# A second product from seven half-size block products, and x held as a ring, in a fused attention and feed-forward kernel

## The chip, the cores and the metric

The kernel runs on one core of one Trainium2 chip. The metric is the device time of one execution in microseconds (us). The engines of the core work side by side and follow each other through semaphores: TensorE (PE) multiplies matrices, VectorE (DVE) and ScalarE (ACT) work elementwise and read the accumulators, GpSimd (POOL) and SyncE (SP) issue most of the transfers. PEld in a profile is PE's weight load.

## The reference, cut to what matters

```
scores = q @ k.T / 8 + bias_table[bucket(|i - j|)]     # 8 batches, 8 heads, 576 positions, 64 wide
x      = softmax(scores) @ v                           # heads side by side: 4608 tokens x 512
h      = x @ w_in                                      # 4608 x 2048
g      = h + sin(alpha * h)**2 / (alpha + 1e-9)
out    = g @ w_out                                     # 4608 x 512
```

Inputs and output are float32; the kernel's operands on PE are float16, its sums float32.

## The kernel before

The work is a list of tasks that `_graph` makes, each with its engine, an estimated duration, what it depends on and what it writes out (`emit`). `_Plan.run` puts them in order, engine by engine. The order on each engine is given ahead of time: `LINE` is a list of task numbers that has been found beforehand, and `_Plan.run` only takes the next task of each engine from it. So each engine has a fixed queue, in which nothing overtakes. `OPT["scalar"]` names the tasks that run on ACT where either ACT or DVE could do them.

Attention goes batch by batch (t = 0 to 7) and head pair by head pair (p = 0 to 3). The two heads of a pair lie in the two halves of the partitions, and their score matmuls (`qk_t`, L1220) use the array as two half arrays of 64 rows that work at the same time. ACT takes the exponential of 1024 columns out of two accumulator banks (`exp_u`, L1228), DVE multiplies in the bias as exp(bias) (`band_t`, L1256), and PE forms the sum over v (`av_w`, L1266 and L1276), with a column of ones for the denominator. `norm` (L1286, L1287) divides, and x is turned to x^T, on PE for t = 0 and by a transposing DMA on SP for the others (`turn_x`, L1293), into the tile `xT`, which holds all 4608 tokens. k and q come in transposed too: for t = 0 and 1, and q of t = 2, by PE (`turn`, L1155) from a staging area that lies inside `xT`, later by transposing DMAs.

The feed-forward part goes by blocks of tokens, `blk`: six of 512, two of 480, one of 576. For each block there are 16 units (f = 0 to 15). A unit is four matmuls `w_in`^T x^T into an accumulator bank (`moe_in`, L1325; two banks for 576 columns), the sine on ACT (`moe_sin`, L1332), the square on ACT or DVE (`moe_sq`, L1337 or L1339), and the gate on DVE (`moe_g`, L1353), which adds h, writes g in float16 and frees the bank. g is kept in buffers of 512 tokens, three of them (`ng=3`).

The second product (`moe_out`, L1368) takes output tiles of 128 tokens in pairs. A tile needs 16 matmuls with 128 columns of g as weights and 512 columns of `w_out` streaming:

```python
r = slice(64 * (i ^ turn), 64 * (i ^ turn) + 64) if rows else slice(0, 128)
self.nc.tensor.matmul(out=c["mo"][i], lhsT=self.g[tau // 4][r, f, at:at + 128],
                      rhs=self.w_out[r, f, :], start=i not in c["began"],
                      stop=True, skip_group_check=True)
```

For the pairs and quarters of f named in `rows`, both tiles are worked on at once, each on one half of the array, so that the array has the same shape as for the score matmuls around them; between the two turns of such a pair DVE touches both banks (`touch`, L1173). The 36 output tiles are copied to SBUF (`evict`, L1305 or L1307) and stored by SP (`store`, L1378).

## Time and profile before

| | us |
|---|---|
| median of 3 runs | 381.75 (381.33 to 381.82) |
| the profiled execution, its own time | 382.92 |
| its span (first to last instruction) | 381.1 |
| first matmul of the whole program | 4.56 |
| first matmul of the first product (block 0) | 35.00 |
| first matmul of blocks 6, 7, 8 | 277.64, 304.12, 329.61 |
| end of the last matmul | 377.44 |

The profile counts an engine as busy while at least one of its instructions runs. A mean per instruction includes its tail, which the next instruction on the engine may cover, so the start-to-start distance in a dense run is the better price; the timeline, which merges runs of equal instructions with their count, gives it. "x408" is a count of instructions.

### The profile page before, as it was taken

The page shows a single profiled execution, that of the slowest core. Times are in us where ns is not written, and L with a number is a line of the kernel's source. Part 1 is how long each engine was busy: PE and PEld are TensorE (multiplying, and loading weights), DVE is VectorE, ACT ScalarE, POOL GpSimd, SP SyncE. Part 2 cuts the span into 40 slices and gives each one's busy share as a digit, 9 for nine tenths or more (in the row PEclk, how much of TensorE's full clock was granted, in tenths as well). Part 3 has the DMA queues.
Part 4 walks back from the last instruction along what each step waited for, and adds up shares of the span by engine and source line. Part 5 has one row for each costly group of instructions (what it writes and reads, how often), then busy time and mean ns, then how long its engine had stood idle before and what let it go on. Part 6 is the DMA issues. An engine that isn't in the chain of part 4 may idle for free.

```text
span 381.1 us, 9520 instructions
## 1 busy us (share of the span) xinstructions
PE 369.9 (97%) x3939; PEld 201.3 (53%) x3939; DVE 268.3 (70%) x635; ACT 314.2 (82%) x419; POOL 88.2 (23%) x105
## 2 busy tenths in 40 slices
PE   4999999999999999999999999999999999999996
PEld 3566445756454556464655465546655545444442
DVE  4686988949964996579748974696569869668402
ACT  4788999899999999999999899997998686557311
POOL 8874651180028201910000008300000000000000
PEclk9999999999999999999999999999999999999999
DMA  8999999499939996997392049941710110210005
GB/s 158 203 157 153 176 186 125 81 148 148 173 82 147 162 158 82 183 157 167 43 182 79 3 96 154 108 67 23 160 58 17 37 37 19 72 57 3 0 2 220
DMA packets 148172, 40.82 MB, mean 107 GB/s; under 512 B 134416, under 2 KB 143456, under 8 KB 148128
## 3 DMA queue, kind: packets, MB, share of 16 engines
q0 software_dynamic: 96656, 18.45, 61.0%
q1 hardware_dynamic: 50768, 21.22, 27.8%
q8 instruction: 31, 0.51, 0.6%
q10 hardware_dynamic: 704, 0.53, 0.6%
q14 instruction: 13, 0.11, 0.1%
HBM read 36.94 MB, written 15.93 MB: 139 GB/s over the span
## 4 chain that ended last, share of the span: by engine, by line
PE 86%; DVE 5%; ACT 3%; DMA 3%; issue 1%; POOL 1%; ACTq 0%; POOLq 0%
PE acc L1368 31%; PE acc L1325 29%; PE acc L1276 10%; PE acc L1220 8%; PE acc L1266 3%; DVE g L1353 2%; ACT u L1228 2%; PE acc L1155 2%; DMA v<-in_v_dram 2%; DMA xT<-in_k_dram 2%; PE acc L1179 2%; PE acc L1210 1%; PE acc L1184 1%; DVE s L1339 1%; DVE xp L1287 1%
## 5 line engine op out<-in xcount | busy, mean ns | idle before, releaser
L1368 PE MATMUL acc<-w_out,g 128*128 128x512 f16 (+1 forms) x744 | 148.0, 378 | 0.6 <-DVE touched L1173 0.5
L1325 PE MATMUL acc<-xT,w_in 128*128 128x512 f16 (+2 forms) x640 | 134.7, 358 | 0.1
L1228 ACT ACTIVATE u<-acc 128x1024 f16<-128x1024 f32 x128 | 123.6, 1038 | 8.0 <-PE acc L1220 6.9
L1332 ACT ACTIVATE s<-acc,alphaT 128x512 f16<-128x512 f32 (+2 forms) x144 | 94.1, 684 | 24.4 <-PE acc L1325 18.2
L1353 DVE SCALAR_TENSOR_TENSOR g<-s,inv_a,acc 128x512 f16<-128x512 f16 (+4 forms) x176 | 107.5, 647 | 9.5 <-ACT s L1337 7.9
L1325 PEld LDWEIGHTS <-w_in 128*128 128x128 f16 x640 | 58.0, 98 | 66.1 <-issue 2.3
L1368 PEld LDWEIGHTS <-g 128*128 128x128 f16 (+1 forms) x744 | 51.2, 96 | 50.7 <-issue 8.4
L1256 DVE TENSOR_TENSOR u<-u,toep 128x1024 f16<-128x1024 f16 (+1 forms) x128 | 59.1, 487 | 26.6 <-ACT u L1228 26.5
L1035 POOL DMA_DIRECT2D v<-in_v_dram x32 | 33.3, 1116 | 91.8 <-PE acc L1276 85.1
L1220 PE MATMUL acc<-qT,kT 64*128 64x256 f16 x512 | 48.1, 285 | 0.5 <-DVE kT L1165 0.5
L1276 PE MATMUL acc<-v,u 128*128 128x65 f16 x1024 | 45.6, 195 | 0.1
L1337 ACT ACTIVATE s<-s 128x512 f16<-128x512 f16 (+2 forms) x70 | 43.2, 630 | 1.2
L1276 PEld LDWEIGHTS <-u 128*128 128x128 f16 x1024 | 41.5, 99 | 4.2 <-issue 0.2
L1307 DVE COPY outs<-acc 128x512 f32<-128x512 f32 x27 | 18.4, 687 | 27.7 <-PE acc L1368 27.2
L1339 DVE TENSOR_TENSOR s<-s 128x512 f16<-128x512 f16 (+2 forms) x74 | 30.2, 419 | 10.2 <-ACT s L1332 10.2
L1220 PEld LDWEIGHTS <-kT 64*128 64x128 f16 x512 | 22.0, 96 | 28.7 <-issue 16.3
L1287 DVE TENSOR_TENSOR xp<-acc,rden 128x256 f16<-128x256 f32 (+1 forms) x64 | 31.4, 491 | 2.4
L1266 PE MATMUL acc<-vt,ut 128*128 128x130 f16 x128 | 28.6, 224 | 0.0
L1041 POOL DMA_DIRECT2D vt<-in_v_dram x16 | 13.3, 832 | 51.8 <-PE acc L1179 27.3
L1305 ACT ACTIVATE outs<-acc 128x512 f32<-128x512 f32 x9 | 5.3, 603 | 18.4 <-PE acc L1368 18.4
L1228 ACT ACTIVATE ut<-acc 128x1024 f16<-128x1024 f32 x16 | 16.5, 1029 | 2.6 <-PE acc L1179 2.0
L1286 DVE RECIPROCAL rden<-acc 128x4 f32<-128x4 f32 (+1 forms) x64 | 11.8, 185 | 9.6 <-PE acc L1276 9.2
(70 smaller groups left out, 231.7 us busy)
## 6 DMA issues: line engine op xcount, KB each, us to landing
out_dram<-outs SPq DMA_DIRECT2D x36, 256.0 KB, 2.5
v<-in_v_dram POOLq DMA_DIRECT2D x32, 128.0 KB, 7.4
staged_k<-in_k_dram POOLq DMA_DIRECT2D x6, 576.0 KB, 11.1
staged_q<-in_q_dram POOLq DMA_DIRECT2D x5, 576.0 KB, 12.9
w_in<-in_moe_w_in_dram POOLq DMA_DIRECT2D x4, 512.0 KB, 8.8
w_out<-in_moe_w_out_dram POOLq DMA_DIRECT2D x4, 512.0 KB, 10.1
xT<-in_q_dram POOLq DMA_DIRECT2D x11, 144.0 KB, 6.5
xT<-in_k_dram POOLq DMA_DIRECT2D x7, 144.0 KB, 6.2
```

The source lines that it names most:

```text
L1220: self.nc.tensor.matmul(out=s[:, o:o + 256], lhsT=self.kT[t % 2][r, p, 128 * c:128 * c + 128], rhs=self.qT[t % 2][r, p, 256 * w:256 * w + ...
L1228: self.nc.scalar.activation(out=c["u"], in_=c["s"], func=AF.Exp, scale=0.125)
L1256: self.nc.vector.tensor_tensor(out=io, in0=io, in1=m, op=ALU.mult)
L1266: nc.tensor.matmul(out=c["av"][:, 130 * j:130 * j + 130], lhsT=tail, rhs=vt[:, p, :], start=True, stop=True, skip_group_check=True)
L1276: nc.tensor.matmul(out=c["av"][:, 130 * j + 65 * a:130 * j + 65 * a + 65], lhsT=l, rhs=vv[:, ch, 2 * p + a, 0:65], start=False, stop=True, ...
L1287: self.nc.vector.tensor_tensor(out=self.ap(x, 256 * w, [[64, n], [1, 64]]), in0=self.ap(av, 0, [[65, n], [1, 64]]), in1=self.ap(r, 0, [[1, ...
L1325: self.nc.tensor.matmul(out=c["h"][:, x:y], lhsT=self.w_in[:, j, 128 * f:128 * f + 128], rhs=self.xT[:, j, lo + x:lo + y], start=(j == 0), ...
L1332: self.nc.scalar.activation(out=c["s"], in_=c["h"], func=AF.Sin, scale=self.alphaT[:, f:f + 1])
L1337: self.nc.scalar.activation(out=c["s"], in_=c["s"], func=AF.Square)
L1339: self.nc.vector.tensor_tensor(out=c["s"], in0=c["s"], in1=c["s"], op=ALU.mult)
L1353: self.nc.vector.scalar_tensor_tensor(out=o, in0=c["s"][:, x:y], scalar=self.inv_a[:, f:f + 1], in1=c["h"][:, x:y], op0=ALU.mult, op1=ALU.add)
L1368: self.nc.tensor.matmul(out=c["mo"][i], lhsT=self.g[tau // 4][r, f, at:at + 128], rhs=self.w_out[r, f, :], start=i not in c["began"], stop ...
```

## The change

For the first eight of nine groups of 512 tokens the second product is formed by blocks. A group's g is 2048 x 512 and `w_out` is 2048 x 512; both are cut in halves in both directions, and the four quarters of the output (256 tokens x 256 columns) come from seven products of quarters instead of eight (Strassen's scheme, in the form with 4 sums on each side). One product is 8 values of f x 2 halves of 128 tokens, so 16 matmuls with 128 columns as weights and 256 columns streaming. The products are numbered; X, Y and Z are three accumulator banks:

- X gets product 1; Y gets product 2; the quarter 11 is X + Y.
- X goes on with product 6; Z gets products 5 and then 3; the quarter 12 is X + Z after both.
- X goes on with product 7; the quarter 22 is X + Z with only 5 in it.
- X goes on with product 4; the quarter 21 is X alone.

X is copied to SBUF after each of the four stages (`quarter`, on ACT or DVE), and the addition of Y or Z is an instruction of DVE on that copy (`quarter_sum`). Four sums of quarters of g are made for each group, in two instructions of 128 x 1024 each (`gate_sum`; two of the four are written over g), and four sums of quarters of `w_out` once (`weight_sum`). The ninth group is done as before, its four tiles one after the other.

To make room, `xT` becomes a ring of 4 x 576 = 2304 tokens, in which batch t writes over batch t - 4. The transposing DMA of x for t of 4 and later waits for the first-product matmuls that read the old tokens. The g buffers are two instead of three, the output buffers of `evict` two instead of three, and there are three buffers for quarters. Staging of q and k moves from `xT` to the tiles of the sums. Blocks are now seven of 512, one of 448 and one of 576; the block that crosses the end of the ring has its matmuls cut in two. `rows` is empty: no second product uses half arrays, and no touches are left. `LINE` is another list throughout, and `scalar` another set: 14 of the 32 copies of quarters are on ACT, of the four copies of the ninth group one is on DVE and three are on ACT, DVE has 84 squares instead of 74, and seven copies of transposed k and q move from DVE to ACT. The planner also knows longer durations for PE in the first 27 us. In the order of PE, five more groups of 12 transposes of q and k come before the first unit of block 0; in that of POOL, seven more loads of q and k, two of `w_out` and two of v come before the last two of `w_in`.

```diff
+XR = 4 * S
...
+        gone = [a for b, l in in_tasks.items() for a in l
+                if BLK[b][0] < S * (t - 3) + 64 and BLK[b][1] > S * (t - 4)] if t > 3 else []
+        tr = add("SP", 1.25, lambda: K.turn_x(xcell, t, p), deps=norms + gone, pipe=1.15, prio=0,
...
+        p1 = product(1, xu, state["fast"] + (in_tasks[bs[-1]][-1:] if bs[-1] == NBLK - 1 else []), g_of(0))
+        p2 = product(2, yu, [], g_of(1))
...
+        c11 = finish(11, p1, yu, p2)[0]
...
+        p5 = product(5, zu, [], both(1, 0))
+        p6 = product(6, None, [c11], both(2, 1))
+        c12 = finish(12, p6, zu, [])
+        p7 = product(7, None, [c12[0]], both(3, 2))
+        c22, q22 = finish(22, p7, zu, p5)
+        p4 = product(4, None, [c22], ww(3))
+        p3 = product(3, None, [q22], lambda f: s_of(4)(f))
+        c12[1].deps.extend(p3)
+        finish(21, p4, None, [])
...
-    line=_line(LINE), rows=((0,0), (0,3), (1,0), (1,1), (1,2), (1,3), (2,3), (3,0), (4,1), (4,3), (5,0), (5,3),
...
+    line=_line(LINE), rows=(), strict=False,
...
-    blk=(512, 512, 512, 512, 512, 512, 480, 480, 576),
+    blk=(512, 512, 512, 512, 512, 512, 512, 448, 576), fast=tuple(range(8)), split=False, p_sum=0.1,
...
-        self.xT = sgl.tile([128, NP, NT + 64], F16, name="xT")
+        self.xT = sgl.tile([128, NP, XR + 64], F16, name="xT")
...
+        self.sums = sgl.tile([128, 2, 2, NF // 2, 256], F16, name="sums")
+        self.wt = sgl.tile([128, 4, NF // 2, 256], F16, name="wt")
...
+        turn = -(-lo // XR) * XR - lo
+        if 0 < turn < n:
+            cuts = sorted({*cuts, turn})
+        for x, y in zip(cuts, cuts[1:]):
+            at = (lo + x) % XR
...
+    def weight_sum(self, i, k):
+        up, low = self.w_out[:, k:k + 4, :], self.w_out[:, k + 8:k + 12, :]
+        out = self.wt[:, :, k:k + 4, :]
+        a, b = ((up[:, :, 256:512], up[:, :, 0:256]), (low[:, :, 256:512], out[:, 0]),
+                (low[:, :, 256:512], up[:, :, 256:512]), (low[:, :, 0:256], out[:, 1]))[i]
+        self.nc.vector.tensor_tensor(out=out[:, i], in0=a, in1=b, op=ALU.subtract)
+
+    def gate_sum(self, c, i, n, k):
+        up, low = self.g[i][:, k:k + 4, :], self.g[i][:, k + 8:k + 12, :]
+        s = self.sums[:, i % 2, :, k:k + 4, :]
+        out, a, b = ((s[:, 0], up[:, :, 256:512], low[:, :, 256:512]), (s[:, 1], s[:, 0], up[:, :, 0:256]),
+                     (up[:, :, 256:512], up[:, :, 0:256], up[:, :, 256:512]),
+                     (low[:, :, 0:256], low[:, :, 0:256], s[:, 1]))[n - 1]
+        self.nc.vector.tensor_tensor(out=out, in0=a, in1=b, op=ALU.add if n == 1 else ALU.subtract)
+
+    def product(self, c, i, n, f0, bank):
+        to = {1: "X", 6: "X", 7: "X", 4: "X", 2: "Y", 5: "Z", 3: "Z"}[n]
...
+        for f in range(f0, f0 + 2):
+            u = f + NF // 2
+            a, b = {1: (g[:, f, 0:256], w[:, f, 0:256]), 2: (g[:, u, 0:256], w[:, u, 0:256]),
+                    5: (s[:, 0, f, :], t[:, 0, f, :]), 6: (s[:, 1, f, :], t[:, 1, f, :]),
+                    7: (g[:, f, 256:512], t[:, 2, f, :]), 4: (g[:, u, 256:512], t[:, 3, f, :]),
+                    3: (g[:, u, 0:256], w[:, u, 256:512])}[n]
+            for k in range(2):
+                self.nc.tensor.matmul(out=c[to][:, 256 * k:256 * k + 256], lhsT=a[:, 128 * k:128 * k + 128],
+                                      rhs=b, start=to not in c["began"], stop=True, skip_group_check=True)
...
+    def quarter(self, c, what, act):
+        c["o", what] = self.tp.tile([128, DM], F32, name="quarter", tag="quarter", bufs=3)
+        self.copy(c["o", what], c["X"], act)
+
+    def quarter_sum(self, c, what):
+        o, b = c["o", what], c["Y" if what == 11 else "Z"]
+        self.nc.vector.tensor_tensor(out=o, in0=o, in1=b, op=ALU.add)
```

236 lines of the change are left out of this document (192 added, 44 removed), and 116 rows, old and new, of the table LINE.

## The prediction

> **What bounds the kernel now.** I read the page first: the busy time of each engine.
>
> ```profile
> span 381.1 us, 9520 instructions
> ...
> PE 369.9 (97%) x3939; PEld 201.3 (53%) x3939; DVE 268.3 (70%) x635; ACT 314.2 (82%) x419; POOL 88.2 (23%) x105
> ```
>
> PE is busy for 97% of the span. A busy PE need not be a full one, so the timeline of PE comes next (columns: start, length of the merged run, engine, line, shapes, count); it says what a matmul costs in a stream.
>
> ```profile
> 35.00 10.30 PE L1325 MATMUL acc<-xT,w_in 128*128 128x512 f16 x47
> ...
> 101.88 0.39 PE L1220 MATMUL acc<-qT,kT 64*128 64x256 f16 x4
> 102.20 2.33 PE L1368 MATMUL acc<-w_out,g 128*128 128x512 f16 x10
> 104.47 0.39 PE L1220 MATMUL acc<-qT,kT 64*128 64x256 f16 x4
> 104.97 0.61 PE L1368 MATMUL acc<-w_out,g 64*128 64x512 f16 x4
> 105.41 0.38 PE L1220 MATMUL acc<-qT,kT 64*128 64x256 f16 x4
> 105.73 0.61 PE L1368 MATMUL acc<-w_out,g 128*128 128x512 f16 x2
> 106.27 0.61 PE L1220 MATMUL acc<-qT,kT 64*128 64x256 f16 x8
> 106.81 0.60 PE L1368 MATMUL acc<-w_out,g 128*128 128x512 f16 x2
> ...
> 107.31 0.41 PE L1276 MATMUL acc<-v,u 128*128 128x65 f16 x8
> 107.55 0.22 PE L1266 MATMUL acc<-vt,ut 128*128 128x130 f16 x1
> ```
>
> Three prices come out of it. The 47 matmuls of 512 columns take 10.30 us, the last one alone some 0.38 us, so they start every (10.30 - 0.38) / 46 = 0.2157 us. The eight of 65 columns start every (107.55 - 107.31) / 8 = 0.030 us. And a change of the array's shape costs about 0.1 us: from 102.20 to 104.47 ten matmuls at 0.2157 leave 0.11 us before the half-array score matmuls; from 105.41 to 105.73 four score matmuls, two at a time, need 2 x 0.109 = 0.22 us of the 0.32. Between the half-array pair of L1368 at 104.97 and the score matmuls at 105.41 there is no such loss: 0.44 us for two pairs. That is what the pairs of the kernel before are for.
>
> The stretches come third. I cut them where PE starts the first product of block 0 (35.00), block 6 (277.64) and block 8 (329.61).
>
> ```profile
> core 0: us, PE busy (x) PEld busy (x) DVE busy (x) ACT busy (x) POOL busy (x), PEclk, DMA share, GB/s
> 0.00:35.00 35.00, 28.42 (x455) 19.30 (x456) 23.76 (x70) 24.85 (x34) 24.98 (x45) 1.00 1.22 174
> 35.00:277.64 242.64, 241.70 (x2778) 132.45 (x2778) 181.19 (x419) 228.65 (x296) 63.26 (x61) 1.00 1.17 123
> 277.64:329.61 51.97, 51.97 (x431) 27.24 (x430) 41.53 (x101) 39.38 (x59) 0.00 (x0) 1.00 0.14 39
> 329.61:381.10 51.49, 47.83 (x277) 22.31 (x275) 21.85 (x47) 21.28 (x32) 0.00 (x0) 1.00 0.16 57
> ```
>
> From 35 us on PE has next to no gap: 0.94 us in the long middle, none after it, until its last matmul 3.7 us before the end. So the time from 35 us is PE's queue, matmul by matmul. But ACT is busy for 228.65 / 242.64 = 94% of the middle too, and only DVE has room there (75%).
>
> **The change, part by part.** I list the forms that carry the costs.
>
> ```profile
> L1368 PE MATMUL acc<-w_out,g 128*128 128x512 f16 x408 | 102.9, 380 | 0.5 <-DVE touched L1173 0.5
> L1353 DVE SCALAR_TENSOR_TENSOR g<-s,inv_a,acc 128x512 f16<-128x512 f16 x112 | 80.2, 743 | 1.2 <-ACT s L1337 0.4
> L1368 PE MATMUL acc<-w_out,g 64*128 64x512 f16 x336 | 45.2, 376 | 0.1
> L1256 DVE TENSOR_TENSOR u<-u,toep 128x1024 f16<-128x1024 f16 x64 | 43.3, 688 | 12.8 <-ACT u L1228 12.8
> L1276 PEld LDWEIGHTS <-u 128*128 128x128 f16 x1024 | 41.5, 99 | 4.2 <-issue 0.2
> L1339 DVE TENSOR_TENSOR s<-s 128x512 f16<-128x512 f16 x51 | 20.7, 420 | 3.8 <-ACT s L1332 3.7
> L1307 DVE COPY outs<-acc 128x512 f32<-128x512 f32 x27 | 18.4, 687 | 27.7 <-PE acc L1368 27.2
> L1287 DVE TENSOR_TENSOR xp<-acc,rden 128x384 f16<-128x384 f32 x32 | 17.8, 558 | 1.3
> L1287 DVE TENSOR_TENSOR xp<-acc,rden 128x256 f16<-128x256 f32 x32 | 13.6, 425 | 1.1
> L1165 DVE COPY qT<-acc 128x576 f16<-128x576 f16 x11 | 8.1, 752 | 6.2 <-PE acc L1155 6.2
> L1305 ACT ACTIVATE xT<-acc 128x320 f16<-128x320 f16 x3 | 1.2, 442 | 0.2 <-PE acc L1300 0.2
> L1163 ACT ACTIVATE kT<-acc 128x576 f16<-128x576 f16 x1 | 0.6, 634 | 0.0
> ```
>
> *Second product on PE.* Before: 408 full matmuls and 336 half-array ones in 168 pairs, so 576 slots of 0.2157 = 124.2 us. After: eight groups of seven products, each 16 matmuls of 256 columns, is 896, and 64 of 512 columns remain for the ninth group. The trace has no full-array matmul of 256 columns. Its price lies between half a 512 slot, 0.108, and a weight load on its own behind it, 0.108 + 0.099 = 0.207. I take the line through 512 columns (0.2157) and 65 columns (0.030): 0.415 ns a column, so 0.109 us, because the 65-column row shows a 128x128 weight load of 99 ns with each matmul and still one start every 30 ns. So 64 x 0.2157 + 896 x 0.109 = 111.5 us, **12.7 us less**.
>
> A rule speaks against this. The Trainium skill, "TensorE: Matmul & The Clock Gate", section "Back-to-back issue gap", gives for streams of weight load and matmul 81 ns at 128 columns and 131 ns at 512: halving a matmul would then save far less than half. On a line between these an estimate for 256 columns is 98 ns, and the sum would be 64 x 0.131 + 896 x 0.098 = 96 us after against 75 us before, 21 us more. This trace disagrees: 0.2157 us at 512 columns, and 0.030 us at 65.
>
> *Changes of shape.* The pairs are given up (rows is empty), so the products stand as full-array work between score matmuls. Counted in the two instruction orders, PE changes its tile shape 146 times before and 192 times after: 46 x 0.1 = **4.6 us more**. All on PE's queue.
>
> *Ring and blocks.* Block 4 crosses the end of the ring, so its 64 matmuls become 128 of 256 columns: 64 x (0.218 - 0.2157) = 0.15 us. Blocks of 480 and 480 become 512 and 448, the same columns. **0.2 us.** The transposed loads of x for t of 4 and later now wait for the matmuls that read the old columns; behind them on SP stand stores and later transposes. PE's order has those matmuls (blocks 0 and 1 for t = 4, up to block 4 for t = 7) one block or more ahead of the av that makes the new x, so this wait is over before it starts: nothing. Without that distance it would hold the next block's first matmuls.
>
> *Two g buffers for three.* A block's first matmul needs the products of the group two before. In PE's order they stand ahead of it, so PE waits for nothing new.
>
> PE's own queue, then: -12.7 + 4.6 + 0.2 = **-7.9 us**.
>
> *Work on DVE.* A row's mean holds a tail that the next instruction covers: in the next fence three gates take 2.06 us, so they start every (2.06 - 0.74) / 2 = 0.66 us where the mean is 0.743; I take 0.08 off each.
>
> ```profile
> 39.84 2.06 DVE L1353 SCALAR_TENSOR_TENSOR g<-s,inv_a,acc 128x512 f16<-128x512 f16 x3
> ```
>
> Added: 64 gate sums and 8 weight sums of 128x1024 f16, nearest row L1256 (0.688, so 0.60 to 0.69; I take 0.60), 43 us; 24 sums of a quarter with an accumulator, 128x512 f32, from the two L1287 rows 0.558 + 0.133 = 0.69, so 0.61 and 15 us. Removed: 8 of 27 copies (5 us), 7 turn copies to ACT (5 us), the nine touches and some split gates (3 us); 10 more squares come (3 us). About +48 us, from 268 to 316. None of it is on PE's chain as long as it is early: each X accumulator is copied out before the next product adds to it, and in PE's order 1.2 to 20 us of other work (mostly over 2 us, by the prices above) stand between a product's last matmul and the next one on X; the copy costs 0.69. Over six blocks the middle gets 48 gate sums, 8 weight sums and 16 quarter sums, less 8 copies and turns and the touches: +37 us, so 218 us. ACT's own list there hardly changes (139 sine and square instructions for 141, 104 exponentials for 106, 5 copies for 3, two turns), about -1 us. PE's work from block 0 to block 5, by the same prices over the two orders, falls by 5.4 us, so the middle would take 237 us: **DVE 92% busy, ACT 96%, PE near 100%**. That fits, but with a slack of 9 us on ACT and 19 on DVE where DVE had 61. I add **1.5 us** for waits this makes on PE, between none (0.94 us stood there at 94% and 75%) and the 17.6 us of the first rival.
>
> *The front.* Five full turn copies of 0.634 and two exponentials of 0.91 (from the next fence, 1.94 less one of 1.03) come ahead of ACT's first sine, three x copies of at most 0.44 go: 5 x 0.63 + 2 x 0.91 - 3 x 0.44 = +3.7 us by counts, against 35.00 - 24.85 = 10 us in which ACT was idle in the first stretch.
>
> ```profile
> 7.67 1.94 ACT L1228 ACTIVATE u<-acc 128x1024 f16<-128x1024 f32 x2
> ...
> 37.32 3.00 ACT L1332 ACTIVATE s<-acc,alphaT 128x512 f16<-128x512 f32 x5
> ```
>
> PE's front gains 2.0 us of work taken from block 0, which is in the sum already. So 0 to 2 us more is open on ACT. POOL's queue has more loads ahead of the last two of w_in, which is the third rival, up to 5 us. Between none and 5 I take **1 us**, nearer to none, since the idle time is there.
>
> *The end.* The stores write rows of half the length, as many bytes; only the last one shows, in the 3.7 us after the last matmul: 0 to 1 us.
>
> **Sum.** -7.9 + 1.5 + 1 = -5.4 us. The profiled execution has a span of 381.1 us and a time of 382.92, 1.2 above the median of the runs, 381.75. So 377.5 against its own time, and **376.4 us** against the median.
>
> **Rivals.** *The DVE queue sets the pace (slower).* Gates free the accumulators for the next first-product unit, and now a sum of 0.60 can stand ahead of a gate. If PE loses 0.2 us at each of the 64 gate sums and 24 quarter sums, that is 17.6 us: 381.75 - 7.9 + 17.6 = 391.5. It decides from 7.9 / 88 = 0.09 us for each. For it: 92% and 96% beside a full PE, no order is that even. Against it: 25% of DVE's middle was idle before and PE lost 0.94 us there with ACT at 94%. Chance 0.16.
>
> *Half-size matmuls don't cost half (slower).* If the weight load showed, 384 more loads x 0.098 = 38 us, so 412 us. The 65-column rows speak against it. Chance 0.01. By the Trainium skill, the same page, section "Part 3: Packing small matmuls", a weight load overlaps running matmuls only in another row group, which would make this so; the trace disagrees, with 30 ns between full-array matmuls.
>
> *Weights of the first product come late (smaller gain).* The DMA engines are full in these first slices of 9.5 us:
>
> ```profile
> DMA  8999999499939996997392049941710110210005
> GB/s 158 203 157 153 176 186 125 81 148 148 173 82 147 162 158 82 183 157 167 43 182 79 3 96 154 108 67 23 160 58 17 37 37 19 72 57 3 0 2 220
> ...
> w_in<-in_moe_w_in_dram POOLq DMA_DIRECT2D x4, 512.0 KB, 8.8
> ```
>
> ```profile
> 23.72 1.51 POOL L1046 DMA_DIRECT2D w_in<-in_moe_w_in_dram  x2
> ```
>
> Ahead of the last two w_in stand seven more loads of q and k of 144 KB, two of w_out of 512 KB and two of v of 128 KB: 2.3 MB, 14 us at 160 GB/s. The last w_in landed near 24.5 + 8.8 = 33.3 us; it is needed by the ninth unit, 8 x 0.86 us after 35, at 42. So 47.3 against 42: up to 5 us of PE in block 0, and 381.75 - 7.9 + 1.5 + 5 = 380.4, if none of these loads fills a gap. Chance 0.13.
>
> *Full gain.* The 2.5 us don't come and half or more of the 46 changes of shape cost nothing: 381.75 - 7.9 - 2.3 = 371.5 and below, down to 369.3 with all of them free. Chance 0.12.
>
> *No effect on the result.* Within 0.2% (about what a measurement of this kernel can tell from no change): gain and waits cancel. Chance 0.03.
>
> **Numbers.** The forecast, 372 to 379, has 0.55. Faster: 0.55 + 0.13 + 0.12 = 0.80; same 0.03; slower 0.17. The range goes from 369.5, the end of the full gain, to 383, the first rival with 0.1 us at each of 88 sums; the rest of the slower cases is left out.
>
> **What would show it.** Right: 896 matmuls of 256 columns starting every 0.109 us; PE busy in the middle still over 98%; DVE there above 90%; the first in-product at 35 to 39 us. Wrong: gaps on PE ahead of in-products released by DVE's gates or sums; ahead of products on X released by quarter copies; a w_in landing in PE's waits near 40 us; a spacing of 256-column matmuls well above 0.11 us.

## The result, and the profile after

The changed kernel takes 385.93 us (median of 6 runs, 384.31 to 387.76), the kernel before on the same chip 381.54 us (380.61 to 383.03). The ratio is 1.0118, with an interval of 1.0078 to 1.0157: 1.2% slower, where 376.4 was forecast, and outside the range of 369.5 to 383.0. The profiled execution has a span of 383.5 us and a time of 385.24. One run each of e1, e8 and e17 below fell into the slower of the chip's two states and is left out of their times.

The page of the changed kernel, its span and the busy time of each engine:

```profile
span 383.5 us, 10185 instructions
...
PE 361.8 (94%) x4219; PEld 241.8 (63%) x4219; DVE 316.8 (83%) x703; ACT 315.0 (82%) x421; POOL 88.5 (23%) x105
```

PE lost 8 us of busy time (369.9 before) and the span still grew by 2.4. So PE now waits. Cut at the first product of blocks 0, 1 and 2, the windows of the changed kernel (same columns as in the prediction):

```profile
0.00:39.09 39.09, 28.42 (x524) 20.27 (x524) 23.85 (x72) 28.77 (x38) 31.58 (x53) 0.91 1.19 161
...
39.09:87.35 48.26, 44.04 (x553) 26.27 (x554) 43.30 (x94) 45.76 (x58) 16.99 (x18) 1.00 1.35 144
87.35:128.22 40.87, 40.02 (x470) 26.19 (x469) 36.02 (x79) 37.04 (x48) 11.49 (x11) 1.00 1.39 143
128.22:383.50 255.28, 249.36 (x2677) 169.12 (x2675) 213.60 (x461) 203.38 (x280) 28.42 (x27) 1.00 0.66 85
```

and of the kernel before, cut at its own blocks 0, 1 and 2:

```profile
35.00:83.95 48.95, 48.64 (x653) 27.44 (x652) 37.68 (x86) 46.66 (x59) 25.64 (x27) 1.00 1.29 139
83.95:116.91 32.96, 32.85 (x374) 17.52 (x373) 26.23 (x63) 32.27 (x44) 5.70 (x7) 1.00 1.37 136
116.91:381.10 264.19, 260.02 (x2461) 137.05 (x2459) 180.66 (x420) 210.38 (x285) 31.92 (x30) 1.00 0.73 89
```

Before, PE is full from 35 us on. After, block 0 has 4.2 us without PE (0.3 before), block 1 has 0.85 (0.1 before), and block 0 starts 4.1 us later. The timeline of PE in the changed kernel names the gaps (idle before the row, and what ended it):

```profile
39.09 3.63 PE L1491 MATMUL acc<-xT,w_in 128*128 128x512 f16 x16 [0.52 <-DVE qT L1327]
...
47.85 3.61 PE L1491 MATMUL acc<-xT,w_in 128*128 128x512 f16 x16 [1.20 <-DVE g L1520]
51.74 4.48 PE L1491 MATMUL acc<-xT,w_in 128*128 128x512 f16 x20 [0.27 <-DVE g L1520]
...
57.89 1.03 PE L1571 MATMUL acc<-w_out,g 128*128 128x256 f16 x8 [0.45 <-DMA w_out<-in_moe_w_out_dram]
...
60.59 0.40 PE L1382 MATMUL acc<-qT,kT 64*128 64x256 f16 x4 [0.79 <-ACT ut L1390]
...
66.41 0.41 PE L1372 MATMUL acc<-qT,kT 64*128 64x64 f16 x16 [0.35 <-ACT u L1390]
...
68.25 0.39 PE L1382 MATMUL acc<-qT,kT 64*128 64x256 f16 x4 [0.40 <-ACT u L1390]
...
88.80 0.59 PE L1491 MATMUL acc<-xT,w_in 128*128 128x512 f16 x2 [0.85 <-DMA xT<-xp]
...
313.88 1.47 PE L1571 MATMUL acc<-wt,sums 128*128 128x256 f16 x12 [1.24 <-ACT quarter L1467]
...
340.15 1.15 PE L1491 MATMUL acc<-xT,w_in 128*128 128x512 f16 x8 [0.31 <-DVE g L1520]
341.56 2.13 PE L1491 MATMUL acc<-xT,w_in 128*128 128x512 f16 x16 [0.26 <-DVE g L1520]
...
372.83 1.91 PE L1571 MATMUL acc<-wt,g 128*128 128x256 f16 x16
```

The last row is the price that the forecast stood on: sixteen matmuls of 256 columns in 1.91 us; less the tail of the last one, 0.273 us (the mean of its form), that is (1.91 - 0.273) / 15 = 0.109 us from start to start.

**The account.** Counts times the prices of the prediction give PE 355.2 us of work before and 347.1 after: -8.1. Block by block, what a stage takes beyond PE's work in it is lost:

| us | PE's work, before | after | lost, before | after | change of the loss |
|---|---|---|---|---|---|
| up to block 0 | 17.9 | 19.9 | 17.1 | 19.2 | +2.1 |
| block 0 | 46.7 | 41.2 | 2.3 | 7.1 | +4.8 |
| block 1 | 32.5 | 39.5 | 0.5 | 1.4 | +0.9 |
| block 2 to the last matmul | 258.2 | 246.5 | 2.3 | 4.8 | +2.5 |
| behind it | | | 3.7 | 3.9 | +0.2 |
| sum | 355.2 | 347.1 | | | +10.5 |

-8.1 + 10.5 = 2.4, the growth of the span. Block 0 is the place: 5.5 us less of PE's work in it (2.0 of them moved ahead of it), and it takes 48.26 us instead of 48.95. Of its +4.8 us, 3.9 are idle time of PE (4.2 against 0.3). Half of the idle time, 2.08 us, stands ahead of rows released by a load or a gate. The other half, 2.07 us in six waits, ends with exponentials of ACT; before the change such waits came to 0.14 us.

**Two chains read back.** The gap at 47.85 ends with a gate. DVE's timeline shows what the gate stood behind:

```profile
45.79 0.69 DVE L1546 TENSOR_TENSOR wt<-w_out 128x1024 f16<-128x1024 f16 x1 [1.74 <-PE acc L1491]
46.40 0.75 DVE L1327 COPY qT<-acc 128x576 f16<-128x576 f16 x1
47.06 2.05 DVE L1520 SCALAR_TENSOR_TENSOR g<-s,inv_a,acc 128x512 f16<-128x512 f16 x3
```

The first weight sum needs the first and the third quarter of `w_out`. It also writes `wt`, which is now the staging area of q and k of t = 1 as well, so it must wait until PE has turned the last of them. The turns were done first: PE waits 0.16 us at 43.25 for their last load and is through with them at 43.95. The third quarter of `w_out`, issued at 33.77, landed at 45.71, and the sum starts at 45.79. POOL's queue, which waits for a landing of `w_out` too, shows both ends:

```profile
33.77 0.81 POOL L1212 DMA_DIRECT2D w_out<-in_moe_w_out_dram  x1
...
45.99 0.62 POOL L1202 DMA_DIRECT2D vt<-in_v_dram  x1 [1.74 <-DMA w_out<-in_moe_w_out_dram]
```

The copy of a turn and three gates wait behind the sum in DVE's queue. So the PE instruction in the sum's brackets is not what it waited for: the cause is a load, and behind it POOL's order of loads.

The gap at 313.88 ends with the copy of a quarter. ACT:

```profile
313.23 0.60 ACT L1467 ACTIVATE quarter<-acc 128x512 f32<-128x512 f32 x1 [1.87 <-PE acc L1491]
```

and SP's queue:

```profile
307.74 1.20 SPq L1455 DMA_TRANSPOSE xT<-xp  x1
309.00 2.97 SPq L1585 DMA_DIRECT2D out_dram<-quarter  x3
```

The copy needs a buffer, there are three, and the three stores that free them were issued behind a transposing load of x that could not go before its x was there. They took 4.1 to 4.2 us to land, the first of them until 309.0 + 4.2 = 313.2, which is when the copy starts.

### The profile page after: what moved, and what is told of

Its sections match the earlier page's. It is cut to its first block, busy times and chain, and to the rows that moved or that the text cites. A ratio compares the mean times of both kernels' runs of the same rounds, so it can differ in the third digit from the quotient of the medians.

```text
span 383.5 us, 10185 instructions
## 1 busy us (share of the span) xinstructions
PE 361.8 (94%) x4219; PEld 241.8 (63%) x4219; DVE 316.8 (83%) x703; ACT 315.0 (82%) x421; POOL 88.5 (23%) x105
## 3 DMA queue, kind: packets, MB, share of 16 engines
q1 hardware_dynamic: 54864, 21.22, 27.5%
## 4 chain that ended last, share of the span: by engine, by line
PE 74%; DVE 8%; DMA 7%; ACT 4%; POOL 3%; issue 2%; SPq 1%; ACTq 0%; DVEq 0%
PE acc L1491 28%; PE acc L1571 23%; PE acc L1438 8%; PE acc L1382 6%; PE acc L1535 4%; DVE g L1520 3%; ACT u L1390 3%; DMA wt<-in_q_dram 3%; PE acc L1428 2%; DMA toep<-e_sb 2%; DMA xT<-xp 1%; DMA cst_sb<-cst 1%; PE acc L1341 1%; DVE u L1418 1%; DVE s L1506 1%
## 5 line engine op out<-in xcount | busy, mean ns | idle before, releaser
L1491 PE MATMUL acc<-xT,w_in 128*128 128x512 f16 (+3 forms) x704 | 134.4, 340 | 3.4 <-DVE g L1520 2.0
L1520 DVE SCALAR_TENSOR_TENSOR g<-s,inv_a,acc 128x512 f16<-128x512 f16 (+2 forms) x160 | 105.7, 689 | 5.0 <-ACT s L1504 2.9
L1491 PEld LDWEIGHTS <-w_in 128*128 128x128 f16 x704 | 64.9, 98 | 59.4 <-issue 3.9
L1571 PEld LDWEIGHTS <-g 128*128 128x128 f16 x640 | 58.6, 98 | 21.2 <-issue 7.8
L1418 DVE TENSOR_TENSOR u<-u,toep 128x256 f16<-128x256 f16 (+1 forms) x128 | 58.8, 486 | 4.1 <-ACT u L1390 3.8
L1196 POOL DMA_DIRECT2D v<-in_v_dram x32 | 33.4, 1117 | 110.8 <-PE acc L1438 46.7
L1571 PE MATMUL acc<-w_out,g 128*128 128x256 f16 x384 | 52.5, 273 | 0.4 <-DMA w_out<-in_moe_w_out_dram 0.4
L1571 PE MATMUL acc<-wt,sums 128*128 128x256 f16 x256 | 35.2, 273 | 1.2 <-ACT quarter L1467 1.2
L1571 PE MATMUL acc<-wt,g 128*128 128x256 f16 x256 | 35.9, 273 | 0.0
L1382 PEld LDWEIGHTS <-kT 64*128 64x128 f16 x512 | 19.2, 96 | 19.1 <-issue 15.7
L1571 PEld LDWEIGHTS <-sums 128*128 128x128 f16 x256 | 23.2, 98 | 10.2 <-issue 5.0
L1581 DVE TENSOR_TENSOR quarter<-quarter,acc 128x512 f32<-128x512 f32 x24 | 16.3, 681 | 5.5 <-PE acc L1571 3.4
## 6 DMA issues: line engine op xcount, KB each, us to landing
staged_q<-in_q_dram POOLq DMA_DIRECT2D x5, 576.0 KB, 13.8
```

Of the source, the lines that this page charges most:

```text
L1196: self.nc.gpsimd.dma_start(out=self.vs[t % 2][:, c, :, 0:D], in_=src)
L1382: self.nc.tensor.matmul(out=s[:, o:o + 256], lhsT=self.kT[t % 2][r, p, 128 * c:128 * c + 128], rhs=self.qT[t % 2][r, p, 256 * w:256 * w + ...
L1418: self.nc.vector.tensor_tensor(out=io, in0=io, in1=m, op=ALU.mult)
L1491: self.nc.tensor.matmul(out=c["h"][:, x:y], lhsT=self.w_in[:, j, 128 * f:128 * f + 128], rhs=self.xT[:, j, at:at + y - x], start=(j == 0 a ...
L1520: self.nc.vector.scalar_tensor_tensor(out=o, in0=c["s"][:, x:y], scalar=self.inv_a[:, f:f + 1], in1=c["h"][:, x:y], op0=ALU.mult, op1=ALU.add)
L1571: self.nc.tensor.matmul(out=c[to][:, 256 * k:256 * k + 256], lhsT=a[:, 128 * k:128 * k + 128], rhs=b, start=to not in c["began"], stop=Tru ...
```

## The experiments

Ratios are against the kernel before on the same chip. A queue is shown by names, and the lines of the diff are its order. Every kernel changes only what is shown; e8, e9, e12, e13 and e15 also hold the accumulator banks of the tasks to a fixed list.

### Is it DVE's new work, and is PE still the pace?

```diff
 e3: gate_sum
-        self.nc.vector.tensor_tensor(out=out, in0=a, in1=b, op=ALU.add if n == 1 else ALU.subtract)
+        return
...
 product
-                    5: (s[:, 0, f, :], t[:, 0, f, :]), 6: (s[:, 1, f, :], t[:, 1, f, :]),
+                    5: (g[:, u, 256:512], t[:, 0, f, :]), 6: (g[:, f, 256:512], t[:, 1, f, :]),
 e4: product
-        for f in range(f0, f0 + 2):
+        for f in [x for x in range(f0, f0 + 2) for _ in range(2 if n == 5 else 1)]:
```

> The changed kernel without its 64 gate sums on DVE (38 us of DVE); products 5 and 6 read blocks of g itself in their place, so the output is not the network's. PE's list is the same. Theory A (the loss lies ahead of 87 us, PE's queue sets the pace behind it): DVE falls from 317 to about 278 us and the time by less than 1 us, to about 385. Theory B (DVE's new work holds PE back): the 6.2 us of PE gaps in blocks 1 to 8 fall to the 2.9 of the kernel before, so 382.5 or less.

> The changed kernel with an eighth product in each of the eight groups: the matmuls of product 5 are issued twice, so 128 more matmuls of 256 columns, and the output is not the network's. At the 0.109 us of the stream this is 14.0 us of PE. If PE's own queue sets the pace from block 0 on (theory A), all of it is seen: 385.9 + 14.0 = 399.9, between 399 and 401. If DVE sets the pace in part (theory B), some of the 14.0 us fills gaps that are there anyway: 3 us less or more, 397 or below.

e3: 386.05 us, ratio 1.0083 (1.0054 to 1.0111). Its page:

```profile
PE 361.9 (94%) x4219; PEld 242.0 (63%) x4219; DVE 280.6 (73%) x639; ACT 315.2 (82%) x421; POOL 87.9 (23%) x105
```

36 us of DVE's work are gone, and with them no time that can be told from noise (the interval overlaps that of the changed kernel). The first rival, the DVE queue, falls as far as the gate sums go; e3 leaves the quarter sums and the weight sums in. e4: 396.51 us, 1.0377 (1.0354 to 1.04). Its 128 added matmuls are 128 x 0.109 = 14.0 us of PE's work; the profiled span grew by 10.9. Most of what PE is given shows, so PE's pace still sets most of the time. Some 1.9 of the missing 3.1 us are gaps that the added work covers: the quarter at 313 us (1.24) and part of the wait for x^T (0.22 for 0.85). Another 0.6 us is a first unit that came earlier, which the edit does not explain. The start of the first unit moves between executions: with the same front it is 39.09 us in the changed kernel, 38.47 in e4, 39.18 in e3 and 39.64 in e14.

### One wait at a time

```diff
 e1: PE, front
-bias_sub, qk_t, qk_t, bias
+qk_t, qk_t, bias_sub, bias
 e2: DVE, block 0
-weight_sum (first), turn copy, gate, gate, gate, ..., sq0.15, weight_sum (second)
+turn copy, gate, gate, gate, ..., sq0.15, weight_sum (first), weight_sum (second)
 e5: POOL
-w_in (second quarter), ..., v, w_in (first quarter), v, w_out, q (t = 1), w_out, w_in, w_in
+w_in (first quarter), ..., w_in (second quarter), k and q (t = 1), w_in, w_in, w_out, w_out, v, v
```

> The changed kernel with one matmul moved: on PE the subtraction of the bias table (L1236), which waits 1.15 us for the landing of cst_sb, stands behind the first two groups of score matmuls instead of ahead of them. Theory A (the gain was lost in the front and in block 0, before 87 us): the first scores start near 6.5 us instead of 7.99, ACT's first exponential near 7.6 instead of 9.07, and the first product of block 0 starts up to 1.5 us earlier than 39.09; the time falls by 0.5 to 1.5 us from 385.9. Theory B (DVE's 48 us of new work holds PE back in blocks 1 to 8): the front gives at most what it gives and blocks 1 to 8 keep their 6.2 us of PE gaps; no more than 1 us. If the band tiles (toep), which come from the same bias chain, are what is late in the front, then this edit makes them later, and the time does not fall.

> The changed kernel with one DVE instruction moved: the first weight sum (L1546 at 45.79 us, which waits 1.74 us for the last turns of t = 1 to leave the tile wt) stands just ahead of the second weight sum, near 58 us. Theory A: the 1.20 us for which PE waits at 47.85 for a gate goes, with part of the 0.27 at 51.74; the time falls by 1.0 to 1.5 us from 385.9. If the gates are late for another reason (ACT's turn copies, w_in), the gap stays and the time changes by less than 0.3 us. Theory B expects no change outside block 0.

> The changed kernel with POOL's queue of loads in another order: the quarter of w_in that block 0 needs first (units 0 to 3) takes the place of the second quarter at 8.71 us; behind the copies of the mask (27.95 us) go first the rest of w_in and the last turns' loads of k and q for t = 1, then w_out, and v of t = 1, needed near 66 us, last. Nothing else moves. Theory A1 (the lost microseconds of block 0 are loads that land late): the waits of PE on wt<-in_q (0.16 us), on the gate behind the weight sum (1.20, which waited for that load), on w_out (0.45) shrink, 1.5 us less at the start of block 1. Theory A2 (each wait removed uncovers the next one, as in the two single moves before this): block 1's first x, the transposes of x for t = 1, still lands at 88.7 to 88.9 us, and the time stays within 0.7 us of 385.9.

e1: 384.86 us, 1.0065 (1.0046 to 1.0084). The first scores start at 6.97 us instead of 7.99, but the first sum over v at 26.40, where it was 26.34. The first unit starts at 38.21; that is not shown to be the edit's work, since e2, with the front as it was, has it at 38.22. Block 1 starts at 87.35 as before, since PE now waits for the load of q:

```profile
43.26 0.70 PE L1318 MATMUL acc<-ident,wt 96*64 96x96 f16 x24 [1.05 <-DMA wt<-in_q_dram]
```

e2: 385.84 us, 1.0093 (1.0076 to 1.0111). The gap of 1.20 us behind the gate is gone, and the two loads that it had covered show:

```profile
47.20 7.08 PE L1492 MATMUL acc<-xT,w_in 128*128 128x512 f16 x32 [0.70 <-DMA w_in<-in_moe_w_in_dram]
56.79 1.03 PE L1572 MATMUL acc<-w_out,g 128*128 128x256 f16 x8 [1.42 <-DMA w_out<-in_moe_w_out_dram]
...
88.66 0.59 PE L1492 MATMUL acc<-xT,w_in 128*128 128x512 f16 x2 [1.83 <-DMA xT<-xp]
```

Block 1's first product started at 86.24, 1.1 us earlier, 0.9 of them because the first unit did; block 0 itself is 0.24 us shorter. The next part of x^T landed at 88.66 (88.80 without the edit). e5: 391.27 us, 1.0244 (1.0215 to 1.0273), worse: `w_out` comes later now, the first weight sum needs its third quarter, and the gates stand behind that sum. DVE and PE of e5:

```profile
48.95 0.69 DVE L1547 TENSOR_TENSOR wt<-w_out 128x1024 f16<-128x1024 f16 x1 [4.57 <-DMA w_out<-in_moe_w_out_dram]
```

```profile
51.02 10.58 PE L1492 MATMUL acc<-xT,w_in 128*128 128x512 f16 x36 [4.78 <-DVE g L1521]
```

So the waits lie in layers: the one removed uncovers the next, and this order of loads is a loss as long as the sum stands early in DVE's queue.

### All of them together, and the stores

e6 is e5, e2 and e1 in one; e7 adds to it:

```diff
 SP, near 305 us
-turn_x (t = 7), store_quarter, store_quarter, store_quarter
+store_quarter, store_quarter, store_quarter, turn_x (t = 7)
 POOL
-staged k of t = 5, ..., two staged loads of t = 3
+two staged loads of t = 3, staged k of t = 5
```

> The order of loads of e5, and the two single moves of before (bias subtraction behind the first scores on PE, first weight sum later on DVE) with it. Theory A1: front -0.9 us, block 0 -1.2 for the gate and -1.5 for loads, so block 1 starts near 84 instead of 87.35; of that 1.5 to 3.5 us reach the end: 382.4 to 384.4. Theory A2: the transposes of x hold block 1 again, as PE's wait there grew from 0.85 to 1.83 us when 1.1 us went ahead of it; then 384.5 to 385.5.

> e6, and on SP the three stores of group 5 that wait behind a transpose of x for t = 7 (issued at 307.74, the stores from 309.00) go ahead of it, so that the quarter buffers come free; on POOL the staging load of k for t = 5 goes behind those of t = 3, out of the way of the transposes of x near 83 us. Theory (the 1.24 us for which PE waits for a quarter copy at 313 is a wait for a buffer whose store landed 4.2 us after its late issue, and not ACT's copy itself): that wait goes, 1.0 to 1.3 us below e6. If it is the copy itself (0.60 us on ACT, behind its exponentials), it stays.

e6: 384.52 us, 1.0083 (1.0056 to 1.0111), where e5 alone had 1.0244. Its block 0 takes 46.99 us, 1.3 less than in the changed kernel. PE's waits for loads and gates there fall from 2.08 to 0.66 us; those for exponentials stay, at 2.04. e7: 383.70 us, 1.0057 (1.0039 to 1.0075). SP of e7 issues the stores at once:

```profile
304.23 1.43 SPq L1586 DMA_DIRECT2D out_dram<-quarter  x3
307.61 1.20 SPq L1456 DMA_TRANSPOSE xT<-xp  x1
```

The gap in front of the quarter product is gone, and block 7 takes 28.40 us instead of 29.55 in e6 and 29.96 in the changed kernel. That chain is shown. It is not gone for good: e10 and e17 have a gap of this kind near 209 us (1.11 and 2.79 us), where the trace of the changed kernel has none.

### The front: copies, clock, and what holds it

```diff
 e8: e7, two turn copies from ACT to DVE
-scalar: ... turn0.1.1 turn0.3.0 ...
 e10: e7, PE, 17 to 25 us: 48 matmuls of 128 columns on the unit matrix into free banks
+fill x6 (ahead of each group of scores that waits for ACT)
 e11: e10 and 27 more ahead of the first transposes, the first scores and the bias product
 e12: e8 and e11, 6 more of these matmuls, and POOL and DVE in the front
-v, v, ..., band, mask, band
+..., v, v, mask, mask, band, band
 e13: e12, POOL
-staged loads of t = 3 behind v
+staged loads of t = 3 ahead of v
```

> e7, and in the front two of the turn copies (0.66 and 0.65 us at 10.9 and 13.1 us of the changed kernel) run on DVE, which idles there, instead of ACT, which is busy without a break from 12 to 25 us while PE waits 0.3 to 0.5 us at each of eight score groups for ACT's exponentials. Theory C (ACT's exponentials set the pace of the front, and the turn copies given to it lengthen them): ACT's stretch ends 1.3 us earlier, the first product of block 0 starts 0.8 to 1.3 us earlier, and as nothing behind block 1 waits for the front any more than before, 0.5 to 1.3 us reach the end: 382.4 to 383.2 at a median of 383.7 for e7. Theory D (the bands on DVE, which wait for the Toeplitz tiles and the masks, set the start of attention times v): the exponentials end earlier, the first matmul with v stays where it is, and so does the time, within 0.4 us.

> e7 with 48 empty matmuls of 128 columns (identity on identity, into a free bank, results unused) on PE in eight of the places where PE waits 0.3 to 0.5 us for ACT between 17 and 25 us, six at each. Theory E (PE's gaps of the front are what takes its clock to a half at about 20 us, for 6.8 us, in some runs for 10.2 us): the clock stays at 1.00 from 13.4 us on, the attention of t = 0 from 25 us on runs at full price sooner, and the first product of block 0 comes 0.5 to 1.5 us earlier; runs near 0.98 of mean clock no longer occur, so the spread of the times shrinks; 382.2 to 383.2. If the halved clock has another cause, it stays, and the time is that of e7, 383.7, or up to 0.5 us more.

> e10 with 27 more of the same empty matmuls ahead of PE's first transposes (from about 3 us, where PE idles until 4.9 to 5.7), ahead of the first scores and ahead of the bias product. Theory E: the clock is full from about 7 to 10 us instead of 13.4, so the transposes and scores up to 13 us, which PE does without a gap at half the speed, take up to 2 us less; ACT's exponentials start to follow each other sooner; the first product of block 0 comes 1 to 2 us earlier than in e7: 381.7 to 382.7. If ACT and the loads hold the front in any case, no gain over e10.

> All that was moved in the front at once: e11 (empty matmuls in PE's gaps), with the two turn copies on DVE (e8), and the loads of v and the bands of p = 0 and 1 moved forward (as in e9). Each of these alone gave 0.4 us or nothing. Theory F (the front has several limits of almost the same length, one behind the other: ACT's exponentials, the clock, the loads of v, the bands on DVE; taking one away shows the next): together they bring the first matmul with v from 25 to 26 us down to 23 to 24 us, the first product of block 0 from 39.1 to 37 to 38 us, and of this 0.5 to 1.5 us reach the end: 381.7 to 382.8. If the front is held by PE and DVE from 26 us on in any case, the time is that of e11, 383.3.

> e12, and on POOL the staging loads of k and q for t = 3 (576 KB each) go ahead of the loads of v that wait for the attention of t = 1, into the stretch from 74 to 80 us in which the DMA engines idle, instead of running beside the transposes of x at 83 to 89 us. Theory G (block 1's first product waits 0.7 to 2.6 us in every kernel for transposes of x that take 4 to 6.6 us from issue to landing because these loads run beside them; undisturbed ones take 2.6): the wait goes, 0.7 to 1.5 us below e12. If the transposes are late by themselves (issued too late), the wait stays, and the store of the first quarters may suffer from the loads beside it: 0 to 2 us more.

The page of the changed kernel shows a granted clock that drops in the front. The windows of the changed kernel:

```profile
13.40:20.30 6.90, 4.53 (x99) 2.82 (x97) 2.27 (x3) 6.90 (x9) 5.84 (x9) 1.00 1.40 226
20.30:27.10 6.80, 5.53 (x57) 3.06 (x57) 5.47 (x13) 5.40 (x7) 6.50 (x13) 0.50 1.46 129
27.10:39.10 12.00, 11.06 (x272) 9.31 (x271) 11.09 (x37) 9.42 (x14) 9.80 (x14) 1.00 1.13 130
```

and of e10:

```profile
13.40:20.30 6.90, 6.10 (x123) 4.08 (x121) 2.27 (x3) 6.90 (x9) 5.54 (x9) 1.00 1.31 218
20.30:27.10 6.80, 4.86 (x79) 3.40 (x78) 5.63 (x13) 5.76 (x7) 6.51 (x13) 1.00 1.49 126
```

ACT is full in the stretch from 13.4 to 20.3 (6.90 of 6.90) with and without the fills. PE is busy there for 66% of the time in pieces with gaps of 0.3 to 0.5 us behind ACT's exponentials, and the clock halves for the next 6.8 us. With the gaps filled it stays at 1.00. The time does not follow: e10 takes 383.68 us, 1.0051 (1.0028 to 1.0074), as e7. e8: 384.94 us, 1.006 (1.0032 to 1.0087), no gain over e7. One more version, e9, is e8 with the orders of POOL and DVE that e12 has, and with the first sum over v three groups of scores earlier. It was expected at 381.5 to 382.5 us and took 384.83, 1.0081 (1.0049 to 1.0113): no gain either. e11: 383.27 us, 1.0044 (1.0029 to 1.0059). e12: 382.39 us, 1.0037 (1.0012 to 1.0063), the best of these. Its first product starts at 36.55 us; how much of that is the edit's work is open, since e13 and e15, with the same front, have 39.47 and 37.21. Two waits for transfers stay on its PE:

```profile
71.38 0.39 PE L1422 MATMUL acc<-qT,kT 64*128 64x256 f16 x4 [0.82 <-DMA kT<-staged_k]
...
86.24 0.59 PE L1531 MATMUL acc<-xT,w_in 128*128 128x512 f16 x2 [1.22 <-DMA xT<-xp]
```

e13 took away both (0.12 us for x^T is left) and is slower all the same: 386.40 us, 1.0148 (1.0101 to 1.0195). Its block 0 takes 50.17 us instead of 47.88, with a wait for x itself at 77.76:

```profile
77.76 0.22 PE L1468 MATMUL acc<-vt,ut 128*128 128x130 f16 x1 [1.85 <-DVE xp L1489]
```

Its first product also comes 2.9 us later than that of e12, with a wait of 2.22 us for a load of k at 25.63 (1.14 us in e12). The edit moves nothing ahead of 57 us, so this part is not shown to be its work.

### Is ACT the pace of block 0 since PE has less to do there?

In block 0 of the changed kernel ACT is busy for 45.76 of 48.26 us, and PE's work is 41.2. e14, e15 (on e12) and e16 (on the kernel before) take ACT's load out of the sines, e17 and e18 (before) out of the exponentials behind them:

```diff
 e14, e15, e16: moe_sin for b == 0 (and no square on ACT there)
-        self.nc.scalar.activation(out=c["s"], in_=c["h"], func=AF.Sin,
+            self.nc.scalar.activation(out=s[:, 512:576], in_=c["h"][:, 0:64], func=AF.Sin,
 e17, e18: exp_u, 24 of them from block 0's first unit on
-        self.nc.scalar.activation(out=c["u"], in_=c["s"], func=AF.Exp, scale=0.125)
+        self.nc.scalar.activation(out=c["u"][:, 0:n], in_=c["s"][:, 0:n], func=AF.Exp, scale=0.125)
```

> The changed kernel with ACT relieved in block 0 alone: the 16 sines of block 0 take 64 of 512 columns (the squares and gates read these again and again), and its four squares on ACT are left out, so the values of block 0 are others; every other instruction, the loads and the order of every queue stay. By the slope of the sine rows (0.83 ns a column) that is 16 x 0.37 + 4 x 0.6 = 8.3 us less for ACT, of the 45.8 us that it is busy in the 48.3 us of block 0. Theory H (block 0 goes at ACT's pace: PE has only 41.2 us of work there since the change, so the 7.4 us that PE lost in this block cannot show): block 0 gets shorter by 4 to 7 us, down to PE's own 41 to 44, and the run with it, 379 to 382 us. Theory W (the loads, the first weight sum and the gates in DVE's queue set block 0): 0 to 1 us, 385 to 386.

> The same relief of ACT in block 0 on the version with the reordered front and the fills (382.4 us; there ACT is busy for 45.8 of the 47.9 us of block 0, and few waits on loads are left). Theory H: block 0 shorter by 4 to 7 us, 376 to 379 us, below the kernel before. Theory W: 0 to 1 us, since what is left of the waits is of another kind.

> The same relief on the kernel before (16 sines of 64 columns, five squares left out: some 9 us less for ACT in block 0). PE is busy there for 48.64 of 48.95 us. Theory H: PE is the bound of block 0 before the change, so nearly nothing, 0 to 1 us, 380.5 to 381.7; with the two runs above this would say that the change moved the bound of block 0 from PE to ACT. If the kernel before gains as much as the changed one, ACT (or what hangs on it) was the bound all along and theory H says nothing on the change.

> The changed kernel with 24 exponentials behind the sines of block 0 taking 512 of 1024 columns; the bias multiplication covers the same half, and the weights of the sum over v are read twice from it, so these values are others. Every matmul, every sine, all loads and the order of every queue stay. A row of 256 columns takes 0.39 us, one of 1024 takes 1.04, so one of 512 some 0.61: 24 x 0.43 = 10 us less for ACT, of 29.65 us that it is busy in the 30.05 us between 57.30 and block 1 (87.35); DVE loses some 5 us there too, and e3, which took 3.5 us from DVE in that stretch, left it at 30.0 us. Theory H2 (not the sines, but the exponentials, back to back, set the pace of this stretch, in which PE lost half of its products' time): the stretch falls to PE's own 25.5 to 27.5 us, 2.5 to 4.5 us less; the run 381.5 to 384, if x^T of t = 1 comes as much earlier. Theory N (neither; PE's waits there are the short way from a score to its own exponential and back): 29 us or more, and 385 to 387.

> The same 24 exponentials at half their columns in the kernel before. From 53.00 to block 1 at 83.95 ACT is busy for 29.05 of 30.95 us and PE for 30.64. Theory H2: PE is the bound there, 0 to 0.5 us less, 380.8 to 381.7. If the stretch falls as much as in the changed kernel, the exponentials were the bound before the change already, and H2 explains no loss.

e14: 386.7 us, 1.0115 (1.0064 to 1.0166); e15: 383.29, 1.0035 (1.001 to 1.0059); e16: 381.69, 1.0004 (0.9985 to 1.0023). Block 0 of e14 in two windows, up to the end of its units and behind them:

```profile
39.64:57.60 17.96, 16.19 (x108) 7.07 (x107) 14.45 (x27) 9.31 (x23) 9.79 (x11) 1.00 1.43 198
57.60:87.68 30.08, 27.86 (x449) 18.93 (x447) 29.36 (x69) 29.63 (x33) 7.18 (x7) 1.00 1.32 106
```

ACT falls from 16.1 to 9.3 us in the first window and block 0 from 48.26 to 48.04 only (e15: 47.88 to 47.05). Theory H falls. The second window had ACT at 29.6 of 30.1 us, hence e17: 387.06 us, 1.0106 (1.0056 to 1.0157), and e18: 381.8 us, 0.9985 (0.9963 to 1.0006). Block 0 of e17 is 2.28 us shorter, 45.98, but 1.35 of that come ahead of 57 us, where the gate's wait was 0.24 instead of 1.20. Behind the wait for `w_out` (at 57.89, in e17 at 56.48) the stretch is 28.52 us instead of 29.46: 0.9 us for the 10 us that ACT was spared. That lies between H2 (25.5 to 27.5) and theory N (29 or more), nearer to N: the exponentials are not the pace of this stretch, but a part of its loss. PE's waits for them in block 0 fall from 2.07 to 1.00 us. In the kernel before the same relief does little, as H2 would have it (block 0 48.63 for 48.95). Block 1 then took 1.5 us of e17's gain back, with 2.33 us where 0.85 stood:

```profile
87.93 0.59 PE L1494 MATMUL acc<-xT,w_in 128*128 128x512 f16 x2 [2.33 <-DMA xT<-xp]
```

## Why the prediction was wrong, point by point

**PE's work: right.** 0.109 us for a 256-column matmul and a sum of -8.1 us against -7.9. PE's busy time fell by 8.1 us. The second rival (half-size matmuls don't cost half, 412 us) is out. Its 384 more loads are a count of slots; the loads of the second product go from 744 to 960. The Trainium skill, "TensorE: Matmul & The Clock Gate", section "Back-to-back issue gap", also has a formula for a single matmul's gap, N / 2.4 + 2.5 ns; that is 109 ns for 256 columns and 216 for 512, and this trace agrees with it, in a stream too, not with the section's 81 and 131 ns (128 and 512 columns).

**Work on DVE: right, and its gate sums harmless.** 316.8 us against 316, and e3 finds no cost of the gate sums. From 39.09 to 282.06 (blocks 0 to 5) DVE is busy for 89%, ACT for 93% and PE for 98%, near the 92, 96 and 100 that were reckoned, and yet this stretch takes 243.0 us where 237 stood. So the 1.5 us of waits in the sum, argued from how full DVE and ACT are over six blocks, stood for the wrong thing: PE's losses are at a few places, each with a chain of its own.

**The waits of PE in block 0 and in the front: the step that failed.** The sum has 1.5 us for waits in the middle and 1 us for the front. Block 0 has no term of its own; only the third rival prices late loads there, at up to 5 us with a chance of 0.13. Measured: +2.1 us lost in the front, +4.8 in block 0, +0.9 in block 1 and +2.5 behind it. The rival read the load rightly and its price wrongly. The quarter of `w_in` for the ninth unit landed at 48.25 us (47.3 was reckoned), but the units came late themselves, so it costs 0.70 us where it shows (e2).

The prediction looked at this one consumer. The late loads have others in block 0: the turns of t = 1 out of `wt`, the products with `w_out`, and the first weight sum, which needs `w_out` and stands ahead of gates in DVE's queue. With these orders mended (e6) block 0 gets 1.3 us shorter. The other half of PE's idle time there, the waits for exponentials, had no term at all. No order of loads moved it (2.05 us in e12), and shorter exponentials halved it (e17). That block 0 lost about as much as the rival's 5 us is therefore luck.

For the front, the 10 us of idle time on ACT was no reason that loads would not be late, with the DMA engines full there; in e3 the first unit waits 0.63 us for its quarter of `w_in`. Which waits make up the 2.1 us is open. The ratio goes from 1.0118 to 1.0083 with the loads, the weight sum and the bias moved (e6), to 1.0057 with the stores (e7) and to 1.0037 with the front (e12). Neighbouring intervals overlap, the first and the last do not.

**"Nothing" for the SP queue and for the cover of X copies: wrong once.** The ring wait was over early, as argued. But "behind them on SP stand stores" was the sentence to follow up: with three quarter buffers the stores are on the path of X. 1.24 us, shown by e7.

**"Two g buffers: PE waits for nothing new": right.** Block 8's first unit, which waits for its buffer, starts at 336.64 without a gap. The gaps of 0.31 and 0.26 us at 340.15 and 341.56 stand ahead of later units of this block, whose 576 columns take two accumulator banks each; a gate ends them. e3, without gate sums, has them too (0.32 and 0.26), and no run removed them.

**Changes of shape, ring and the end** fit the account (3.9 us behind the last matmul, 3.7 before); no run prices them one by one.

**What stays open.** By the ratio e12 is 1.4 us slower than the kernel before, where 5.4 us of gain were forecast. Its profiled execution (span 379.4) puts the rest in block 0 again, 47.88 us for 41.2 of work, 4.4 us more lost than before the change. In e6 to e9 block 0 takes 47.0 us. The gaps of e12 there are small: 0.82 us for a staged k, 2.05 in seven waits for exponentials, 0.7 for gates. That the missing cover is the reason is argued, not shown: before, 16 full and 96 half-array matmuls of 512 columns (13.8 us) of the second product stood in block 0, and now 80 of 256 columns (8.7 us). That ACT's load as such is not the pace is shown by e14 to e18. Which of the front's waits is last after e12 was not settled either.

## What to carry to other kernels

Work saved on a full engine is time only where the engine had nothing else to wait for: make the sum stage by stage, and in each ask what the removed work was covering. When new work goes into a queue ahead of old work (here a weight sum ahead of gates, a transpose ahead of the stores out of three buffers), follow everything it needs back through every queue to its load, and compare the releaser that a trace names with when that releaser was done. A wait in a trace is the top layer: price the ones below it before changing an order, or the change may cost more than it brings (e5).

## What the runs showed of the hardware

- Gaps of 0.3 to 0.5 us on PE at 66% busy were followed by a granted clock of 0.50 over the next 6.8 us; with 48 small matmuls in the gaps it stayed at 1.00 (e10). The Trainium skill, "TensorE: Matmul & The Clock Gate", section "A second HAM failure mode: psum-queue depth-cycling", says that short idle times of PE between groups of matmuls can make the clock swing between full and half; these two runs agree.
- The clock in the records is not the whole price. In the kernel before it reads 1.00 throughout, and yet four scores take 0.61 us early and 0.39 later:

```profile
21.56 0.61 PE L1220 MATMUL acc<-qT,kT 64*128 64x256 f16 x4
...
30.38 0.39 PE L1220 MATMUL acc<-qT,kT 64*128 64x256 f16 x4
```

  In the changed kernel the same four take 0.61 us where a clock of 0.50 is recorded, and 0.39 at 1.00:

```profile
24.18 0.61 PE L1382 MATMUL acc<-qT,kT 64*128 64x256 f16 x4 [0.15 <-ACT u L1390]
...
29.16 0.39 PE L1382 MATMUL acc<-qT,kT 64*128 64x256 f16 x4
```

  So the kernel before seems to run its front at half the speed too, unrecorded. Its sums over v say until when:

```profile
25.01 0.65 PE L1276 MATMUL acc<-v,u 128*128 128x65 f16 x8
...
27.08 0.41 PE L1276 MATMUL acc<-v,u 128*128 128x65 f16 x8
```

  The changed kernel pays the lower price from 13.49 us on (0.39 for four scores) until its recorded drop at 20.3; the kernel before pays the higher one until some time between 25.0 and 27.1. So the recorded drop alone is no sign that the change lost time to the clock.

- The six runs of the changed kernel group by mean clock: three at 0.989 to 0.991 took 384.3 to 385.2 us, three at 0.980 to 0.981 took 386.6 to 387.8, while the kernel before stays at 0.998 to 1.000. That the clock makes the difference within the six is not shown: in e3 runs at 0.991 took 384.0 to 386.8 us. e10, at 0.997 to 1.000 and still 1.0051, shows that the loss is not the clock's alone.
- The part of x^T of t = 1 that block 1 waits for landed at 88.80, 88.66 and 87.93 us in the changed kernel, e2 and e17, though block 1 came up to 2.3 us earlier, and at 90.64 in e3, where block 1 came at 87.42. Why it does not move with the work was not settled.
